# Double weights to float32: two VectorE passes in place of three

## The chip, the cores and the metric

The kernel runs on one core of a Trainium2 chip. The metric is the device time of one execution in microseconds (us); the time given is the median of three runs.

## The reference

Attention with a memory term, and behind it two feed-forward layers (called FFN here) with 2304 tokens, 512 channels and 2048 hidden columns. The weights of both layers come as doubles, everything else as float32.

```python
def reference(**kwargs):
    attn_out = _attn_ref(**attn_kwargs)                # 4 batches, 8 heads, 576 tokens, 64 wide
    B, H, S, D = attn_out.shape
    x = np.ascontiguousarray(attn_out.transpose(0, 2, 1, 3)).reshape(B * S, H * D)
    x = _moe_ref(x=x, **moe_kwargs)                    # h = x @ w_in; g = h * cos(h); g @ w_out
    return _moe2_ref(x=x, **moe2_kwargs)               # h = x @ w_in; g = h * tanh(softplus(h)); g @ w_out
```

## The kernel before

The work is cut into three parts. Attention goes over 4 batches of 4 head pairs, and each pair takes five query blocks, called steps here (80 in all). A step has a stage a (scores `sp` at L238 and L251, row minimum and mask on VectorE at L240, exp on ScalarE at L243, the reciprocal at L263, scaling at L265 on GpSimd in the first batch), a stage b two steps later (transposes `tp` at L297 and their copies `aT`), and a stage c four steps later (`o` at L313 and L324). Once per pair `memory` computes `mp` (L277), `den` (L280, L281) and `mo` (L282). When the first batch is done, units of the first layer's first half (columns of hidden, 24 matmuls `h` at L420, then cos, then 24 matmuls `y` at L478) are put between the attention steps. cos is taken for two units at once (L367, L368, L372, L375) and needs another activation table than the exp of attention, so each pair of units brings two table loads on ScalarE. After attention come the second half of the first layer, and then the second layer (`y` at L487).

The weights come in 64 pieces of 128 x 512 doubles, in four groups of 16: `w0` (needed by the units among the attention steps), `w1`, `w2` and `w3`. The function `to_f32` turns a piece into float32: a load into `wst` (two buffers), a scaling of the high words on GpSimd (the kind "ws" of `scaled`, L119), a rounding of the low words on ScalarE (L128), and three passes on VectorE (L129, L130, L133). Then `load_half` splits the float32 into a high and a low part, by a copy on ScalarE or GpSimd (L115, L119) and a subtraction on VectorE or GpSimd (L163). Of `w0` one piece is loaded at the start, and the rest from step 14 of attention on, at a rate of 0.9 pieces a step.

A scheduler of the language sets the order of the instructions on each engine, by its own estimate of their times; each engine then works through its list in order. A change of one instruction can so move others.

Of the kernel before, what the change touches and what calls it, by code (L numbers as in the profile page):

```python
# [9 lines left out]
F32 = mybir.dt.float32  # L10
F32R = mybir.dt.float32r
I32 = mybir.dt.int32
U32 = mybir.dt.uint32
AF = mybir.ActivationFunctionType
ALU = mybir.AluOpType
# [22 lines left out]


REBIAS = 2.0 ** -112  # L40


@with_exitstack
def attention_moe_moe_kernel(
# [14 lines left out]
    nc = tc.nc  # L59
    P = 128  # L60
# [21 lines left out]
    const = ctx.enter_context(tc.tile_pool(name="const"))  # L82
# [15 lines left out]
    nc.vector.reciprocal(gate, igate)  # L98
    nc.vector.tensor_scalar(omg, gate, -1.0, 1.0, ALU.mult, ALU.add)

    c_seven = const.tile([P, 1], F32, name="c_seven")
    nc.gpsimd.memset(c_seven, 7.0)

    counts = {}

    def turn_of(kind, first=False):
# [5 lines left out]
    def scaled(kind, dst, src, scale=1.0, first=False):  # L112
        eng = turn_of(kind, first)
        if eng is nc.scalar:
            eng.activation(dst, src, AF.Copy, scale=scale)  # L115
        elif scale == 1.0 and eng is nc.vector:
            eng.tensor_copy(dst, src)
        else:
            eng.tensor_scalar(dst, src, scale, 1.0, ALU.mult, ALU.mult)  # L119

    def to_f32(src, dst=None):


        st = wk.tile([P, SM, 2], I32, tag="wst", name="wst", bufs=BUFS["wst"])
        nc.sync.dma_start(st, src)
        lo, hi = st[:, :, 0], st[:, :, 1]
        scaled("ws", hi.bitcast(F32), hi.bitcast(F32), REBIAS)
        nc.scalar.activation(lo, lo.bitcast(U32), AF.Relu, scale=-(2.0 ** -29), bias=c_seven)  # L128
        nc.vector.scalar_tensor_tensor(lo, hi, 3, lo, ALU.logical_shift_left, ALU.bitwise_or)  # L129
        nc.vector.tensor_scalar(hi, hi, -(1 << 31), 7, ALU.bitwise_and, ALU.bitwise_or)  # L130
        if dst is None:
            dst = lo
        nc.vector.tensor_tensor(dst, lo, hi, ALU.bitwise_xor)  # L133
        return dst.bitcast(F32)

    def weight_pieces(win, wout, half, tl):
# [30 lines left out]
    def from_double(win, wout, half):  # L167
        def f(tl):
            for src in weight_pieces(win, wout, half, tl):
                yield to_f32(src)  # L170
        return f
# [495 lines left out]
```

## Time and profile before

| | |
|---|---|
| time, median of 3 runs (lowest, highest) | 1070.43 us (1069.86, 1070.5) |
| span of the profiled execution, first to last instruction | 1068.0 us |
| the median less the span | 2.4 us |
| TensorE (PE) busy | 1042.6 us, 98% |
| VectorE (DVE) busy | 490.7 us, 46% |
| ScalarE (ACT) busy | 485.8 us, 45% |
| GpSimd (POOL) busy | 391.6 us, 37% |

The page gives no time of its own for the profiled execution, only its span; its whole time is taken as that of the runs, the span and some 2.4 us around it. Busy shares are means over parts with different limits, so the rows below look at stretches.

### The profile page before, as it was taken

How to read it: one execution, taken by the hardware profiler on the slowest of the kernel's cores; microseconds unless marked ns; L12 is line 12 of the kernel's file. 1: busy time of each engine (PE TensorE's matmuls, PEld its weight loads, DVE VectorE, ACT ScalarE, POOL GpSimd, SP SyncE). 2: the span in 40 equal slices, each digit the busy share in tenths (PEclk: the TensorE clock that was granted, in tenths of full speed). 3: DMA queues.
4: the chain of work that ended last, by engine and by line, in shares of the span. 5: the costliest groups of instructions: out<-in, count | busy, mean ns of one | idle time of the engine just before them, and what ended most of it. 6: DMA issues, size and time to landing. Idle time of an engine off the chain costs nothing.

```text
span 1068.0 us, 17139 instructions
## 1 busy us (share of the span) xinstructions
PE 1042.6 (98%) x6512; PEld 873.7 (82%) x6512; DVE 490.7 (46%) x1136; ACT 485.8 (45%) x1023; POOL 391.6 (37%) x425
## 2 busy tenths in 40 slices
PE   6997999999999999999999999999999999999998
PEld 4666688787878899998888889888888888888897
DVE  4588885445554558776766655665000000000000
ACT  6797875556564534344535454543322321222131
POOL 3377853323232334555555555654101010110100
PEclk8999999999999999999999999999999999999999
DMA  6366642323121275425345355630300300110010
GB/s 235 119 196 224 205 135 82 119 83 122 59 87 46 73 266 190 139 90 198 110 166 177 111 176 185 228 119 22 116 1 1 118 1 0 60 40 1 21 41 20
DMA packets 66369, 116.99 MB, mean 110 GB/s; under 512 B 5616, under 2 KB 25072, under 8 KB 66288
## 3 DMA queue, kind: packets, MB, share of 16 engines
q1 hardware_dynamic: 66288, 115.91, 32.2%
q8 instruction: 51, 0.84, 0.3%
q14 instruction: 30, 0.25, 0.1%
HBM read 87.58 MB, written 28.31 MB: 109 GB/s over the span
## 4 chain that ended last, share of the span: by engine, by line
PE 92%; ACT 2%; DVE 2%; DMA 2%; issue 1%; POOL 1%; SPq 0%; DVEq 0%; POOLq 0%; ACTq 0%
PE h L420 37%; PE y L478 20%; PE y L487 18%; PE o L324 5%; PE sp L238 4%; PE tp L297 4%; PE o L313 2%; PE mp L277 1%; PE sp L251 1%; DMA qt<-in_qp_dram 1%; DMA wst<-in_w1i_dram 1%; DVE at L240 1%; ACT at L243 1%; DMA vt<-in_vn_dram 1%; POOL at L265 0%
## 5 line engine op out<-in xcount | busy, mean ns | idle before, releaser
L420 PE MATMUL h<-xbH,w 128*128 128x256 f32 (+1 forms) x1536 | 393.0, 338 | 0.1
L420 PEld LDWEIGHTS h<-xbH,w 128*128 128x128 f32 x1536 | 266.9, 190 | 33.7 <-issue 1.0
L420 PE MATMUL h<-xbL,w 128*128 128x256 f32 (+1 forms) x768 | 258.0, 336 | 1.5 <-DMA xbL<-xsL 1.5
L478 PE MATMUL y<-g,w 128*128 128x256 f32 (+1 forms) x1344 | 221.5, 319 | 4.4 <-ACT aT L115 4.2
L478 PEld LDWEIGHTS y<-g,w 128*128 128x128 f32 x1344 | 193.1, 192 | 30.8 <-issue 9.4
L487 PE MATMUL y<-w,g 128*128 128x512 f32 x864 | 201.8, 389 | 0.0
L487 PEld LDWEIGHTS y<-w,g 128*128 128x128 f32 x864 | 161.9, 188 | 33.5
L392 DVE TENSOR_TENSOR g<-e,g 128x512 fp32r<-128x512 f32 x36 | 24.9, 691 | 297.1 <-ACT g L115 297.1
L420 PEld LDWEIGHTS h<-xbL,w 128*128 128x128 f32 x768 | 145.6, 190 | 16.9 <-DMA xbL<-xsL 1.7
L392 POOL TENSOR_TENSOR g<-e,g 128x512 fp32r<-128x512 f32 x36 | 47.8, 1328 | 286.5 <-ACT g L115 286.5
L265 POOL TENSOR_SCALAR at<-at,sm,omg 128x128 f32<-128x128 f32 (+2 forms) x144 | 102.7, 723 | 134.4 <-DVE sm L263 119.2
L384 ACT ACTIVATE e<-h 128x512 f32<-128x512 f32 x72 | 43.0, 597 | 232.5 <-PE h L420 231.0
L392 POOL TENSOR_TENSOR g<-u,g 128x512 fp32r<-128x512 f32 x72 | 102.0, 1436 | 121.5 <-ACT g L115 45.6
L367 ACT ACTIVATE u<-h 128x512 int32<-128x512 f32 x72 | 42.9, 595 | 111.9 <-PE h L420 104.2
L243 ACT ACTIVATE at<-at,mn 128x128 f32<-128x128 f32 (+3 forms) x128 | 70.9, 555 | 28.2 <-DVE mn L240 26.8
L129 DVE SCALAR_TENSOR_TENSOR wst<-wst 128x512 int32<-128x512 int32 x64 | 53.9, 843 | 37.7 <-POOL wst L119 31.3
L119 POOL TENSOR_SCALAR wst<-wst 128x512 f32<-128x512 f32 x64 | 46.4, 731 | 63.2 <-DMA wst<-in_w1i_dram 25.1
L297 PE MATMUL tp<-ident,at 128*128 128x128 f32 x384 | 63.9, 285 | 5.6 <-DVE den L281 2.2
L368 DVE SCALAR_TENSOR_TENSOR u<-u,h 128x512 f32<-128x512 int32 x72 | 49.0, 682 | 40.8 <-ACT u L367 40.5
L240 DVE CUSTOM_DVE_ANT_0 at<-sp,mask 128x128 f32<-128x128 f32 (+3 forms) x128 | 59.3, 482 | 17.6 <-PE sp L238 16.0
L133 DVE TENSOR_TENSOR wst<-wst 128x512 int32<-128x512 int32 x64 | 66.1, 1035 | 1.2
L324 PE MATMUL o<-aT,vt 128*64 128x128 f32 (+1 forms) x896 | 64.5, 272 | 1.7 <-ACT aT L115 1.5
(76 smaller groups left out, 1084.1 us busy)
## 6 DMA issues: line engine op xcount, KB each, us to landing
wst<-in_w1i_dram SPq DMA_DIRECT2D x16, 512.0 KB, 5.4
wst<-in_w1o_dram SPq DMA_DIRECT2D x16, 512.0 KB, 4.6
wst<-in_w2i_dram SPq DMA_DIRECT2D x16, 512.0 KB, 4.0
wst<-in_w2o_dram SPq DMA_DIRECT2D x16, 512.0 KB, 4.7
qd<-in_qT_dram SPq DMA_DIRECT2D x16, 320.0 KB, 3.4
vt<-in_vn_dram SPq DMA_DIRECT2D x16, 320.0 KB, 3.2
xbH<-xsH SPq DMA_DIRECT2D x20, 256.0 KB, 4.9
xbL<-xsL SPq DMA_DIRECT2D x20, 256.0 KB, 4.6
```

Of the source, the lines that this page charges most:

```text
L129: nc.vector.scalar_tensor_tensor(lo, hi, 3, lo, ALU.logical_shift_left, ALU.bitwise_or)
L133: nc.vector.tensor_tensor(dst, lo, hi, ALU.bitwise_xor)
L240: nc.vector.tensor_tensor_reduce(at[:, :N], sp[:, :N], mask[:, SM - q0:SM - q0 + N], SSC, 3.0e38, ALU.add, ALU.min, mn[:, j:j + 1])
L243: marks["act"] = nc.scalar.activation(at[:, :N], at[:, :N], AF.Exp, bias=mn[:, j:j + 1], scale=-1.0, accum_out=sm[:, j:j + 1]).ins
L265: turn_of("sc", b == 0).tensor_scalar(at[:, :N], at[:, :N], sm[:, j:j + 1], gates[j], ALU.mult, ALU.mult)
L297: nc.tensor.transpose(tp[:, c:c + P], at[:, c:c + P], ident)
L324: marks["pe"] = nc.tensor.matmul(o[j * D:(j + 1) * D, :n], st["vt"][:kk, c, j * D:(j + 1) * D], a, start=False, stop=c == i, skip_group_ch ...
L368: nc.vector.scalar_tensor_tensor(u, u.bitcast(I32), -TWO_PI, h, ALU.mult, ALU.add)
L392: turn_of(kind).tensor_tensor(gL, g, gH.bitcast(F32), ALU.subtract)
L420: nc.tensor.matmul(h[:, a * T:(a + 1) * T], w_[:, c, f0:f0 + P], x_[c], start=m == 0, stop=m == 3 * NC - 1)
L478: nc.tensor.matmul(y[e // per][:, cols], w_[:, f, es], g_, start=fst and m == 0 and e % per == 0, stop=lst and m == 2, skip_group_check=True)
L487: nc.tensor.matmul(y[t], g_[:, tsl], w_[:, f, :], start=fst and m == 0, stop=lst and m == 2, skip_group_check=True)
```

## The change

The old form makes the complement of the three low mantissa bits (ScalarE: 7 less the low word, clamped at zero by Relu, rounded to an integer), ORs it with the shifted high word, makes a word with the sign and the number 7 from the high word, and XORs the two. The new form has ScalarE round the low word itself, scaled a little down so that it stays within 7; then one VectorE pass ORs the sign to it, and a second ORs the shifted high word. The pass at L130 goes, with the constant tile `c_seven`; the ScalarE operation is Copy with numbers for scale and bias where it was Relu with a bias tile.

```diff
+LOW = 29.0 / 32.0
...
-    c_seven = const.tile([P, 1], F32, name="c_seven")
-    nc.gpsimd.memset(c_seven, 7.0)
...
-        nc.scalar.activation(lo, lo.bitcast(U32), AF.Relu, scale=-(2.0 ** -29), bias=c_seven)
-        nc.vector.scalar_tensor_tensor(lo, hi, 3, lo, ALU.logical_shift_left, ALU.bitwise_or)
-        nc.vector.tensor_scalar(hi, hi, -(1 << 31), 7, ALU.bitwise_and, ALU.bitwise_or)
+        nc.scalar.activation(lo, lo.bitcast(U32), AF.Copy, scale=LOW * 2.0 ** -29, bias=0.2495)
+        nc.vector.scalar_tensor_tensor(lo, hi, -(1 << 31), lo, ALU.bitwise_and, ALU.bitwise_or)
         if dst is None:
             dst = lo
-        nc.vector.tensor_tensor(dst, lo, hi, ALU.bitwise_xor)
+        nc.vector.scalar_tensor_tensor(dst, hi, 3, lo, ALU.logical_shift_left, ALU.bitwise_or)
         return dst.bitcast(F32)
```

In the changed kernel the lines behind `to_f32` have numbers lower by 3: L420 is L417, L368 is L365, L163 is L160. The ScalarE rounding is L126, the two passes are L127 and L130. The scheduler's order differs on all engines from step 14 of attention to about step 35, and little after that: the matmuls of steps 36 to 80 stand as before but for a few.

The first place is TensorE's list where the first FFN units enter (`h` of unit one is made with the weight tiles `w_90` and `w_91` before, `w_88` and `w_89` now; unit two before with `w_94` and `w_95`). Before:

```order
L238 MATMUL sp<-kd,qd 128x256 x2
L238 MATMUL sp<-kd,qd 128x384 x2
L238 MATMUL sp<-kd,qd 128x512 x2
L420 MATMUL h<-xbH,w_90 128x256
L420 MATMUL h<-xbL,w_90 128x256
...
L251 MATMUL sp<-kd,qd 128x512
L251 MATMUL sd<-kd,qd 128x64
L420 MATMUL h<-xbH,w_94 128x256
```

Now:

```order
L417 MATMUL h<-xbH,w_88 128x256
L417 MATMUL h<-xbL,w_88 128x256
...
L294 MATMUL tp<-ident,at 128x128 x6
L310 MATMUL o<-ident,mo 128x128
L321 MATMUL o<-aT,vt 64x128 x4
L235 MATMUL sp<-kd,qd 128x384
L294 MATMUL tp<-ident,at 128x128 x8
L274 MATMUL mp<-mz,ph 128x130 x5
L310 MATMUL o<-ident,mo 128x128
```

Before, all 48 matmuls of the first two units stand between the `o` of step 21 and that of step 23. Now the first 6 (on the first half of the channels) stand there, the other 18 of unit one by step 27, and unit two at steps 32 and 33. By step 35 both lists have 72 `h` matmuls.

The second place is VectorE's list where the first `u` of cos and a pair's `mo` meet. Before:

```order
L133 TENSOR_TENSOR wst<-wst 128x512
L129 SCALAR_TENSOR_TENSOR wst<-wst 128x512
L281 RECIPROCAL den<-den 128x6
L280 SCALAR_TENSOR_TENSOR den<-mp,igate 128x4
L368 SCALAR_TENSOR_TENSOR u<-u,h 128x512
L130 TENSOR_SCALAR wst<-wst 128x512
L163 TENSOR_TENSOR w_97<-wst,w_96 128x512
L282 TENSOR_TENSOR mo<-mp,den 128x384
```

Now:

```order
L277 SCALAR_TENSOR_TENSOR den<-mp,igate 128x6
L278 RECIPROCAL den<-den 128x6
L365 SCALAR_TENSOR_TENSOR u<-u,h 128x512
L277 SCALAR_TENSOR_TENSOR den<-mp,igate 128x4
L279 TENSOR_TENSOR mo<-mp,den 128x384
L260 RECIPROCAL sm<-sm 128x1
```

Before, three weight passes and a split stand between the first `den` and `mo`; now none does.

The third place is ScalarE's list at the first cos (the sine with its table load). Before:

```order
L217 ACTIVATE ph<-qt 128x576
L328 ACTIVATE xH<-o 128x128
L218 ACTIVATE ph<-ph 128x576
L372 ACT_TABLE_LOAD
L372 ACTIVATE u<-u,c_hpi 128x1024
L115 ACTIVATE aT<-tp 128x512
```

Now:

```order
L126 ACTIVATE wst<-wst 128x512
L240 ACTIVATE at,sm<-at,mn 128x256
L214 ACTIVATE ph<-qt 128x576
L369 ACT_TABLE_LOAD
L369 ACTIVATE u<-u,c_hpi 128x1024
L325 ACTIVATE xH<-o 128x128
L126 ACTIVATE wst<-wst 128x512
L215 ACT_TABLE_LOAD
L215 ACTIVATE ph<-ph 128x576
L240 ACTIVATE at,sm<-at,mn 128x256
L113 ACTIVATE aT<-tp 128x512
```

The first cos came with step 23 and comes with step 33 now; the number of table loads is the same, and behind the sine stands the exp of the next pair's `ph`, with a rounding of weights ahead of it, before the copy `aT`.

## Rows read from the trace of the kernel before

**Rows 1.** The page's first part: busy us (share of the span) and instructions.

```profile
PE 1042.6 (98%) x6512; PEld 873.7 (82%) x6512; DVE 490.7 (46%) x1136; ACT 485.8 (45%) x1023; POOL 391.6 (37%) x425
```

**Rows 2.** Windows, cut at the ends of head pairs: length, busy us by engine, granted clock, DMA.

```profile
35.00:50.20 15.20, 15.20 (x122) 9.93 (x122) 7.44 (x34) 11.37 (x38) 5.51 (x9) 1.00 0.36 109
50.20:69.20 19.00, 18.27 (x147) 12.60 (x148) 14.98 (x51) 15.77 (x48) 10.55 (x14) 1.00 0.60 203
69.20:83.30 14.10, 13.68 (x119) 9.24 (x117) 13.06 (x48) 12.50 (x38) 11.90 (x13) 1.00 0.64 200
83.30:111.10 27.80, 22.37 (x180) 18.30 (x180) 22.28 (x69) 20.12 (x50) 20.12 (x22) 0.94 0.66 222
111.10:127.70 16.60, 15.18 (x126) 10.34 (x124) 16.50 (x56) 13.18 (x40) 12.53 (x15) 1.00 0.55 179
127.70:145.30 17.60, 17.33 (x151) 13.71 (x152) 15.68 (x51) 14.10 (x40) 13.58 (x16) 1.00 0.53 177
145.30:400.00 254.70, 250.52 (x2125) 213.16 (x2124) 134.25 (x433) 139.71 (x344) 80.65 (x102) 0.99 0.32 106
400.00:1068.00 668.00, 664.09 (x3395) 569.55 (x3394) 248.88 (x327) 235.39 (x362) 224.38 (x194) 1.00 0.27 93
...
1050.00:1075.00 25.00, 14.35 (x77) 12.11 (x75) 0.69 (x1) 3.65 (x6) 1.28 (x1) 0.94 0.06 21
```

**Rows 3.** Windows of line L130 alone: length, DVE busy (instructions), clock, DMA.

```profile
480.00:650.00 170.00, 19.55 (x16) 1.00 0.45 155
```

**Rows 4.** Chain that ended last, 155 to 170 us: start, us, what.

```profile
162.84 2.88 PE h L420 x24
```

**Rows 5.** Waits of TensorE, 83 to 112 us: total us, times, longest.

```profile
PE tp L297 <- DVE den L281: 2.2, 1, 2.2
PE h L420 <- DMA xbL<-xsL: 1.5, 1, 1.5
PE o L313 <- ACT aT L115: 0.9, 1, 0.9
```

**Rows 6.** Windows, 104 to 108 us: columns as in rows 2.

```profile
104.00:106.00 2.00, 1.17 (x6) 0.95 (x8) 2.00 (x5) 1.99 (x4) 1.40 (x2) 0.71 0.47 137
106.00:108.00 2.00, 2.00 (x19) 1.67 (x16) 2.00 (x7) 0.28 (x1) 1.45 (x2) 0.50 0.22 47
```

**Rows 7.** Groups by line of VectorE, 50 to 150 us: busy us, mean ns, idle before.

```profile
L133 DVE TENSOR_TENSOR wst<-wst 128x512 int32<-128x512 int32 x16 | 12.5, 784 | 0.1
L129 DVE SCALAR_TENSOR_TENSOR wst<-wst 128x512 int32<-128x512 int32 x16 | 11.6, 723 | 2.8 <-POOL wst L119 2.3 <-ACT wst L128 0.6
L130 DVE TENSOR_SCALAR wst<-wst 128x512 int32<-128x512 int32 x16 | 9.5, 594 | 0.0
```

**Rows 8.** The tile wst: duration ns min/median/max, first and last start.

```profile
L130 DVE TENSOR_SCALAR wst<-wst x64: 404/654/1543, 57.5 to 735.1; 128x512 int32<-128x512 int32 x64
L133 DVE TENSOR_TENSOR wst<-wst x64: 678/732/1790, 57.9 to 735.6; 128x512 int32<-128x512 int32 x64
```

**Rows 9.** Groups by line of ScalarE, 50 to 150 us: columns as in rows 7.

```profile
L128 ACT ACTIVATE wst<-wst,c_seven 128x512 int32<-128x512 uint32 x16 | 12.3, 772 | 3.0 <-DMA wst<-in_w1o_dram 1.6 <-DMA wst<-in_w1i_dram 1.4
...
L115 ACT ACTIVATE w<-wst 128x512 fp32r<-128x512 f32 x8 | 5.4, 679 | 4.2 <-DVE wst L133 4.2
```

**Rows 10.** Timeline of VectorE, 96 to 104 us: start, us, what.

```profile
100.18 0.68 DVE L129 SCALAR_TENSOR_TENSOR wst<-wst 128x512 int32<-128x512 int32 x1
...
101.51 0.42 DVE L130 TENSOR_SCALAR wst<-wst 128x512 int32<-128x512 int32 x1
101.85 0.68 DVE L163 TENSOR_TENSOR w<-wst,w 128x512 fp32r<-128x512 f32 x1
102.45 0.55 DVE L282 TENSOR_TENSOR mo<-mp,den 128x384 f32<-128x384 f32 x1
```

**Rows 11.** Timeline of ScalarE, 88 to 112 us: start, us, what, idle before.

```profile
101.85 1.28 ACT L372 ACT_TABLE_LOAD   x1
103.14 1.15 ACT L372 ACTIVATE u<-u,c_hpi 128x1024 f32<-128x1024 f32 x1
```

## The prediction

> **What bounds the kernel now.** The page's first part says TensorE: 98% busy, VectorE 46% [rows 1]. A share of the span hides where the two meet, so the next view is the windows, cut at the ends of head pairs [rows 2]. From 400 us on TensorE is busy for 664.09 of 668.00 us, and 3.65 of the missing 3.91 us lie behind its last matmul: it stops at 1064.35 us (14.35 us into the last window), and the span ends at 1068.0. Three of the four groups of weights are converted in that stretch. Between 480 and 650 us, for instance, the 16 passes of L130 take 19.55 us of VectorE [rows 3], over twice what 16 take early, and TensorE loses nothing by it. So 48 of 64 pieces are hidden behind matmuls, and their saving is worth zero; if that cover were gone, VectorE would set the pace there, but it is busy for 248.88 of those 668 us and loses work by the change. From 145.30 to 400 us no weights are converted; the 4.18 us that TensorE idles there stand, since its order there is kept.
>
> What is left is the five head pairs from 50.20 to 145.30 us, in which the 16 pieces of `w0` are converted among attention steps. In these windows VectorE is busy for 82.5 of 95.1 us (14.98 + 13.06 + 22.28 + 16.50 + 15.68), 87%, and TensorE idles 0.73 + 0.42 + 5.43 + 1.42 + 0.27 = 8.27 us. The pair before, without weight passes, takes 15.20 us with VectorE at 7.44 us, 49%, and TensorE never idle. Five such pairs and the 72 `h` matmuls that the order puts among them (24 take 2.88 us [rows 4]) would be 76.0 + 8.6 = 84.6 us, 10.5 less than the 95.1 us that they take. Idle time makes 8.27 of this. Most of the rest is the clock: the granted clock fell to 0.71 from 104 to 106 us and to 0.50, its lower level of 1.2 GHz, from 106 to 108 [rows 6], behind the waits of [rows 5]; that costs 2.00 x 0.29 + 2.00 x 0.50 = 1.58 us. **At stake are 8.27 + 1.58 = 9.85 us**, and 5.43 + 1.58 of it in the one window from 83.30 to 111.10 us. The waits there name a VectorE instruction of `den` (2.2 us), a load of `xbL` (1.5) and a copy `aT` (0.9) [rows 5]. VectorE worked without a gap then: between the two `den` and the `mo` that TensorE needed stood L129, L130 and the split L163, 0.60, 0.34 and 0.60 us from start to next start [rows 10] (for L129 its 0.68 us less the overlap of 0.08 that L163 shows). Behind them ScalarE's table load and sine (1.28 + 1.15 us [rows 11]) kept `aT` back.
>
> **The change, part by part.** (a) *The pass L130 goes*: 16 in the stretch at a mean of 594 ns, 9.5 us of VectorE [rows 7]. The Trainium skill (VectorE: DVE Perf Modes, The perf-mode tier table) speaks against so much: a float32 operation with one tensor source in SBUF runs at twice the rate of one with two, so the pass that goes would be the cheapest of the three. The trace agrees for its fastest, 404 ns against 678 for L133 [rows 8]; by it alone the saving would be 16 x 0.404 = 6.5 us and the gain under (e) 0.2 us smaller. I take the mean, since passes are stretched up to 1.5 us in place.
>
> (b) *XOR of two tensors becomes shift-and-OR*: the trace has no such second pass. Its nearest rows are L133 itself (784 ns) and L129, the same form (723) [rows 7]: 16 x 0 to 0.061 = 0 to 1.0 us. I take 1.0, as the form is L129's.
>
> (c) *ScalarE's rounding without a bias tile*: bounded by 772 ns as now and by the 679 ns of the Copy at L115 on the same tile [rows 9]: 0 to 1.5 us of 16. I take 1.5, the like operation; ScalarE has room, so it counts for the latency of a piece only. GpSimd's scaling and the loads stay as they are; the memset of `c_seven` goes before the first matmul has its data, and counts nothing.
>
> (d) *Latency*: from ready words to the float32 piece, three passes of 723 + 594 + 784 ns become two of 723 at most 784 ns: 0.65 us less, so one of the two `wst` buffers and the next load come as much earlier.
>
> (e) *Worth of the VectorE time*: 82.5 - 9.5 - 1.0 = 72.0 of 95.1 us, 76%. TensorE's idle time goes with VectorE's load: nil at 49%, 8.27 us at 87%. On a line between the two, 76% gives 8.27 x 27 / 38 = 5.9 us, a fall of 29%. In the four quieter windows (0.73 + 0.42 + 1.42 + 0.27 = 2.84 us) that is **0.8 us**. The bounds are 0 (idle time set by other engines) and 2.84.
>
> (f) *The order at the first units*. The scheduler, with shorter conversions, no longer puts 48 `h` matmuls, both `u`, the sine and three conversions into one pair. The second half of `xbL` is needed three steps later, some 9 us at 15.20 us for five: the 1.5 us wait goes. `mo` now stands ahead of the weight passes: 0.60 + 0.34 + 0.60 = 1.5 of the 2.2 us wait go. The wait for `aT` may stay or move with the sine. That is **3.0 us**. With the idle stretch so cut, the clock may or may not fall; I count half of 1.58, **0.8 us**. Bounds: 0, if as much idle time turns up at step 33, and 5.43 + 1.58 = 7.01.
>
> Sum: 0.8 + 3.0 + 0.8 = 4.6 us, between 0 and 9.85. The profiled span is 1068.0 us and the runs' median 1070.43, so 2.4 us lie around the span and stay. **1070.43 - 4.6 = 1065.8 us.**
>
> **Rivals.** *Hidden anyway.* VectorE is at 46% and TensorE at 98%: what is gone from VectorE was never on the path, and the early waits are a matter of loads and of table loads, which the change doesn't touch. For it: 48 of 64 pieces are hidden so, and one of three waits named is a DMA. Against: VectorE's 87% in the five pairs, and the passes between `den` and `mo`. It gives 0.8 us or less, 1070 us. The Trainium skill (Perfetto Trace Analysis, Identifying the Most-Contended Engine) says to work on the engine with the highest occupancy first, which would here be TensorE; by it nothing is gained. The trace bears this out from 145 us on and not before.
>
> *The stall moves and grows (slower).* Around the first sine ScalarE now has, in order, a rounding of weights, a table load, the sine, `xH`, another rounding, a second table load and the exp of `ph`, ahead of the next exp of scores. If the load of either piece comes late, ScalarE stands with the scores' exp behind it, VectorE's `sm` and GpSimd's scaling wait for that, and TensorE for the scaled rows. Priced by the stall that is there now, 5.43 + 1.58 us, plus the 1.28 + 1.15 us of load and sine that the six `h` matmuls left at step 23 no longer cover, against 7.0 us that go with the old place: +2.4 us, 1072.9. It decides where the piece lands later than TensorE's filler lasts (24 `h`, 2.88 us). For it: TensorE had 48 `h` matmuls (5.8 us) at the old place and stalled still. Against: the order has unit three close behind, and VectorE has less to do.
>
> *Everything goes.* With VectorE at 76% the five pairs run as the undisturbed one: 9.85 us less, 1060.6. Against: each pair with weights has some idle time, and the table loads stay.
>
> *No cheaper in fact*: two two-source passes stretched as L133 is (784 ns) instead of three: 16 x 0.061 = 1.0 us of VectorE less saved; by (e) under 0.1 us, inside the forecast.
>
> **The numbers.** The forecast holds with 0.48 (1062 to 1068.2), everything goes with 0.12, hidden 0.27 (1068.3 to 1072), slower 0.13 (1072.6 and up, centred at 1072.9 and open above). A difference of 0.2%, 2.1 us, is about what a measurement of this kernel can tell from none. So faster has 0.60, same 0.27, slower 0.13. The range leaves out the far half of everything-goes and most of slower: 1061.2 to 1072.0.
>
> **What would show it.** In the trace of the changed kernel: 16 pairs of passes of some 0.7 us each and VectorE near 72 us in the stretch up to step 35 ((a), (b)); the rounding near 0.68 us (c); TensorE's idle time from 50 us to step 35 at 4 to 5 us in place of 8.3 (e, f); no wait for `xbL` at the first units, and the clock at 1.00 or a shorter fall (f); from there on every matmul earlier by the same amount to the end. I am wrong if the idle time is as large at another place, such as the sine at step 33, if the clock falls twice, or if the 4.18 us of idle time from 145.30 to 400 us change, which I hold fixed.

## The result and the profile after

The changed kernel takes 1080.86 us (median of 5 runs, 1079.3 to 1082.22) where the kernel before, run beside it, takes 1070.5 (5 runs, 1069.86 to 1073.4): a ratio of 1.0088, with a 95% interval of 1.0072 to 1.0105. It is slower by 0.9%, outside the predicted range. The profiled execution has a span of 1079.6 us, 11.6 longer. Every median here is of runs within 1.5% of the fastest of their kernel; one run of 2594 us (the changed operations in their own order with two places, below) is left out so, and with it that median would be 1081.77 us in place of 1080.29. In the changed kernel the load of a piece is L123, and the `y` matmul of L478 is L475.

The page's first part, the line that answers to [rows 1], columns as there:

```profile
PE 1049.2 (97%) x6512; PEld 876.3 (81%) x6512; DVE 452.8 (42%) x1072; ACT 480.3 (44%) x1023; POOL 392.2 (36%) x424
```

VectorE lost 37.9 us of work, as the edit promised, and the kernel still got longer. Where, the windows of the changed kernel show, cut at the ends of the same head pairs (for [rows 2]), and in steps of 2 us behind 466 us (for [rows 6]):

```profile
36.20:51.40 15.20, 15.20 (x122) 9.95 (x121) 7.42 (x34) 11.36 (x38) 6.05 (x9) 1.00 0.41 131
51.40:69.50 18.10, 18.10 (x147) 12.75 (x146) 13.51 (x50) 14.84 (x46) 9.84 (x13) 1.00 0.59 180
69.50:87.60 18.10, 14.17 (x110) 9.01 (x111) 14.60 (x47) 13.77 (x42) 12.81 (x14) 0.96 0.57 187
87.60:106.20 18.60, 18.60 (x143) 13.86 (x142) 14.15 (x45) 11.30 (x34) 11.56 (x17) 0.86 0.73 238
106.20:125.00 18.80, 17.33 (x140) 11.91 (x139) 17.15 (x56) 15.02 (x46) 15.18 (x17) 1.00 0.56 182
125.00:149.70 24.70, 23.28 (x169) 17.63 (x168) 19.34 (x58) 17.85 (x44) 15.35 (x17) 0.93 0.53 166
149.70:176.80 27.10, 26.47 (x227) 22.64 (x226) 15.20 (x48) 14.37 (x35) 10.85 (x14) 1.00 0.36 115
...
400.00:1079.60 679.60, 671.35 (x3439) 576.11 (x3437) 216.24 (x285) 232.83 (x363) 229.03 (x196) 1.00 0.29 94
...
466.00:468.00 2.00, 0.98 (x9) 0.78 (x7) 2.00 (x4) 0.73 (x2) 1.27 (x2) 1.00 0.03 8
468.00:470.00 2.00, 0.31 (x1) 0.19 (x1) 2.00 (x3) 0.00 (x0) 0.97 (x2) 1.00 0.10 10
470.00:472.00 2.00, 1.04 (x8) 0.99 (x8) 1.84 (x3) 0.13 (x1) 1.64 (x2) 0.96 0.78 208
472.00:474.00 2.00, 2.00 (x11) 2.00 (x11) 1.41 (x2) 1.97 (x4) 1.84 (x2) 0.50 0.86 306
474.00:476.00 2.00, 2.00 (x14) 2.00 (x14) 1.97 (x4) 0.23 (x1) 0.39 (x2) 0.69 0.58 168
```

Two things are to be seen. The long window of the kernel before, 27.80 us, shrank to 18.60 (part of its matmuls stand in later windows now), but the window ahead of it grew from 14.10 to 18.10 with 3.93 us of idle TensorE, and the clock is below 1.00 in three windows where it was in one (two falls, the first from 86 to 94 us and the second from 144 to 148). And the stretch that the prediction called hidden has a hole: from 466 to 472 us TensorE works 2.33 of 6 us, and then the clock stands at 0.50 and 0.69. The waits of TensorE name who was late, from 50 to 177 us (first four lines, for [rows 5]) and from 440 to 480 us (last two), columns as there:

```profile
PE tp L294 <- POOL at L262: 2.6, 4, 1.1
PE sp L235 <- ACT aT L113: 1.7, 2, 0.9
PE o L321 <- ACT aT L113: 1.5, 1, 1.5
PE sp L235 <- DVE mn L237: 0.9, 1, 0.9
...
PE y L475 <- DVE g L115: 2.7, 1, 2.7
PE y L475 <- POOL g L389: 1.0, 1, 1.0
```

Setting the n-th matmul of each kind beside the n-th of the kernel before, the changed kernel is 1.3 us behind at 25 to 60 us, 7.0 at 175, 5.2 from 213 (the kernel before runs at a clock of 0.88 and 0.78 from 200 to 210 us, the changed one does not), 4.4 at 450, 10.1 from 480 and 11.7 from 745 us to the end.

The groups by line of the stretch from 50 to 150 us, VectorE for [rows 7] and ScalarE for [rows 9]:

```profile
L130 DVE SCALAR_TENSOR_TENSOR wst<-wst 128x512 int32<-128x512 int32 x15 | 12.6, 837 | 0.0
L127 DVE SCALAR_TENSOR_TENSOR wst<-wst 128x512 int32<-128x512 int32 x15 | 12.1, 809 | 7.2 <-POOL wst L117 5.0 <-ACT sm L259 1.9 <-ACT wst L126 0.2
...
L126 ACT ACTIVATE wst<-wst 128x512 int32<-128x512 uint32 x16 | 10.8, 678 | 8.8 <-DMA wst<-in_w1i_dram 3.8 <-DMA wst<-in_w1o_dram 3.4 <-POOL at L262 1.5
```

The rounding is as short as forecast (678 ns), but ScalarE now waits 7.2 us in these 16 for the load of the words, where it waited 3.0 us [rows 9]. That is the first hint of the cause: the loads come later. The piece at 460 us shows it in full, in the timelines of the changed kernel by engine (start, duration, instruction, idle time before it):

```profile
457.89 1.64 POOL L160 TENSOR_TENSOR w<-wst,w 128x512 fp32r<-128x512 f32 x1
...
459.15 0.93 DVE L160 TENSOR_TENSOR w<-wst,w 128x512 fp32r<-128x512 f32 x1 [0.80 <-ACT w L113]
...
460.14 0.37 SPq L123 DMA_DIRECT2D wst<-in_w1i_dram  x1
...
463.95 0.69 ACT L126 ACTIVATE wst<-wst 128x512 int32<-128x512 uint32 x1 [3.86 <-DMA wst<-in_w1i_dram]
464.53 1.15 ACT L369 ACTIVATE u<-u,c_hpi 128x1024 f32<-128x1024 f32 x1
...
466.41 1.27 DVE L372 TENSOR_TENSOR u<-h,u 128x512 f32<-128x512 f32 x2
467.61 1.60 DVE L127 SCALAR_TENSOR_TENSOR wst<-wst 128x512 int32<-128x512 int32 x1
...
469.69 0.35 PE L475 MATMUL y<-g,w 128*128 128x256 f32 x1 [2.71 <-DVE g L115]
```

Both splits of the pieces ahead have ended at 459.53 and 460.08 us; the next load is issued at 460.14 and lands some 3.8 us later; ScalarE has the rounding of that piece ahead of the sine L369 in its list and stands for 3.86 us; the product at L372, the cast `g` and TensorE's `y` are late in turn. VectorE adds to it: between that product and the cast stands the pass L127 of the next piece, 1.60 us long here.

In the early stretch the trace is less plain. The load issued at 77.48 us lands at 82.63; ScalarE has stood for 1.55 us and begins the rounding at 82.71, with an exp and the copy `aT` behind it, for which TensorE waits 1.5 us. But a scaling of `at` on GpSimd that the same rounding waits for ends at 82.65, so this wait alone does not tell which of the two cost the time. The experiments have to.

### The profile page after: what moved, and what is told of

Read it like the earlier page. It is cut to its first block, busy times and chain, and to the rows that moved or that the text cites. A ratio compares the mean times of both kernels' runs of the same rounds, so it can differ in the third digit from the quotient of the medians.

```text
span 1079.6 us, 17195 instructions
## 1 busy us (share of the span) xinstructions
PE 1049.2 (97%) x6512; PEld 876.3 (81%) x6512; DVE 452.8 (42%) x1072; ACT 480.3 (44%) x1023; POOL 392.2 (36%) x424
## 4 chain that ended last, share of the span: by engine, by line
PE 77%; DMA 8%; DVE 6%; ACT 5%; POOL 3%; issue 2%; SPq 0%; POOLq 0%; ACTq 0%; DVEq 0%
PE h L417 30%; PE y L475 16%; PE y L484 15%; PE o L321 4%; PE sp L235 4%; PE tp L294 3%; DMA wst<-in_w1o_dram 2%; DMA wst<-in_w2o_dram 2%; DVE wst L127 2%; PE o L310 1%; DVE wst L130 1%; DMA wst<-in_w1i_dram 1%; PE mp L274 1%; DMA wst<-in_w2i_dram 1%; ACT at L240 1%
## 5 line engine op out<-in xcount | busy, mean ns | idle before, releaser
L417 PE MATMUL h<-xbH,w 128*128 128x256 f32 (+1 forms) x1536 | 392.8, 338 | 0.0
L417 PEld LDWEIGHTS h<-xbH,w 128*128 128x128 f32 x1536 | 267.2, 190 | 33.0 <-issue 1.2
L417 PE MATMUL h<-xbL,w 128*128 128x256 f32 (+1 forms) x768 | 258.2, 337 | 0.0
L475 PE MATMUL y<-g,w 128*128 128x256 f32 (+1 forms) x1344 | 221.3, 319 | 8.5 <-ACT aT L113 4.2
L475 PEld LDWEIGHTS y<-g,w 128*128 128x128 f32 x1344 | 193.0, 192 | 34.6 <-issue 11.9
L417 PEld LDWEIGHTS h<-xbL,w 128*128 128x128 f32 x768 | 145.9, 190 | 15.3 <-issue 0.2
L389 DVE TENSOR_TENSOR g<-e,g 128x512 fp32r<-128x512 f32 x36 | 25.9, 718 | 299.2 <-ACT g L113 268.6
L389 POOL TENSOR_TENSOR g<-e,g 128x512 fp32r<-128x512 f32 x36 | 47.3, 1313 | 281.2 <-ACT g L113 281.2
L389 POOL TENSOR_TENSOR g<-u,g 128x512 fp32r<-128x512 f32 x72 | 103.3, 1452 | 99.0 <-DVE g L115 40.9
L117 POOL TENSOR_SCALAR wst<-wst 128x512 f32<-128x512 f32 x64 | 46.8, 731 | 138.8 <-DMA wst<-in_w2o_dram 40.7
L365 DVE SCALAR_TENSOR_TENSOR u<-u,h 128x512 f32<-128x512 int32 x72 | 49.0, 682 | 65.1 <-ACT u L364 64.8
L127 DVE SCALAR_TENSOR_TENSOR wst<-wst 128x512 int32<-128x512 int32 x64 | 54.4, 851 | 44.5 <-POOL wst L117 41.6
L235 PE MATMUL sp<-kd,qd 64*128 64x128 f32 (+3 forms) x256 | 65.5, 495 | 7.0 <-DMA kd<-in_kT_dram 4.5
L126 ACT ACTIVATE wst<-wst 128x512 int32<-128x512 uint32 x64 | 43.0, 674 | 64.7 <-DMA wst<-in_w1i_dram 17.0
```

What stands on the lines that cost most here:

```text
L127: nc.vector.scalar_tensor_tensor(lo, hi, -(1 << 31), lo, ALU.bitwise_and, ALU.bitwise_or)
L235: nc.tensor.matmul(sp[:, :N], st["q"][rows, q0:q0 + P], st["k"][rows, :N], start=True, stop=True)
L365: nc.vector.scalar_tensor_tensor(u, u.bitcast(I32), -TWO_PI, h, ALU.mult, ALU.add)
L389: turn_of(kind).tensor_tensor(gL, g, gH.bitcast(F32), ALU.subtract)
L417: nc.tensor.matmul(h[:, a * T:(a + 1) * T], w_[:, c, f0:f0 + P], x_[c], start=m == 0, stop=m == 3 * NC - 1)
L475: nc.tensor.matmul(y[e // per][:, cols], w_[:, f, es], g_, start=fst and m == 0 and e % per == 0, stop=lst and m == 2, skip_group_check=True)
```

## The experiments

### Is it the order?

First theory: the operations are cheaper as meant, and the scheduler's new order costs the time. To test it, an order can be written out: behind the traced program each instruction of an engine is tied behind the one that is to stand ahead of it there. The ranks come from the built programs of the two kernels, without or with the pass at L130.

```diff
         attention_moe_moe_kernel(tc, *args)
+        in_order(tc)
...
+        for d in ranks[at:at + len(mine)]:
+            r += d
+            want.append(mine[r])
+        for a, b in zip(want, want[1:]):
+            tc.add_manual_dep(b, a.name, mybir.DependencyInfo(mybir.DependencyClass.NoSync, mybir.DependencyReason.DATA), reason="order")
```

The changed operations in the order of the kernel before:

> The changed kernel's operations, with the order of the kernel before written out for all five engines (every instruction behind the one that stood ahead of it there; the sign pass left out). If the new order is what cost the time (theory), this run shows the operations alone: 1064 to 1068 us, and neither the idle 2.7 us for the cast g at 470 us nor the idle 3.9 us of TensorE at 69 to 88 us comes back. If the new operations themselves cost it (rival: the two-source passes stretched beside GpSimd, or a shorter VectorE chain that shifts the bursts), it stays at 1078 to 1082.

Measured: 1069.45 us, ratio to the kernel before 0.9982 (0.9972 to 0.9992), a little above the range expected. The operations as such cost nothing.

The old operations in the changed kernel's order:

> The operations of the kernel before (Relu, three VectorE passes), with the order of the changed kernel written out for all five engines; the sign pass stands right behind the first pass. Theory (order): slow like the changed kernel or slower, 1078 to 1086 us, since the same order now carries 38 us more of VectorE work, and TensorE waits for g at 460 to 476 us. Rival (operations): 1068 to 1073, as before.

Measured: 1094.55 us, 1.0212 (1.0192 to 1.0232), slower than the range expected. Up to here the theory holds. The two orders agree on all engines between TensorE's instructions 893 and 2460, so that the first part can be taken from one and the rest from the other:

> The changed kernel's operations; the order of the kernel before up to where both orders coincide (TensorE's instruction 1500, about 260 us), its own order behind that. Theory: the loss of about 5.6 us between 50 and 165 us goes and that at 460 to 476 us (about 5.7) and at 725 to 750 us (1.6) stays: 1073 to 1076 us. If the first loss belongs to the operations: 1079 to 1082.

> The reverse: the changed kernel's own order up to TensorE's instruction 1500 (about 260 us), the order of the kernel before behind that. Theory: the idle time and the lower clock at 466 to 476 us and the wait at 725 to 750 us go (5.7 + 1.6 us), those at 50 to 165 us stay: 1072 to 1075 us. If the later losses belong to the operations: 1079 to 1082.

Measured: 1069.3 us, 0.9980 (0.9966 to 0.9994), and 1072.66 us, 1.0011 (0.9999 to 1.0023). The theory falls with the first of them. It has the changed kernel's order at 460 and at 745 us, and neither loss is there: TensorE is busy for 40.00 of 40 us from 440 to 480. Either half of the old order takes that loss away, so it isn't a property of the order at that place. Something that the kernels of longer time share had to be looked for.

It is the loads of the pieces. The numbers are from the traces: the issue of the n-th load less the end of the split of piece n - 2, in us, for six of the 64 pieces (counted from 0).

```
piece             14      20      25      29      31      63
before         -3.25   -6.10  -12.44  -11.02   -8.14   -8.74
changed        +0.03   +0.07   +0.03   +0.61   +0.03   +0.03
```

In the changed kernel every load waits for the split two pieces ahead of it; before, loads go out up to 22 us ahead of it: 50 of 60 by more than 1 us, and the other 10 within about 1 us of its end. The built programs say why. The 64 staging tiles `wst` stand at these addresses of a partition (and so many tiles at each):

```
before     82048 (18)  86144 (17)  90240 (15)  94336 (14)
changed    82048 (33)  86144 (31)
```

The code asks for two buffers (`bufs=2`) in both. That number steers the scheduler's plan; what the loads wait for on the chip, by the issue times above, is the reuse of an address, and the placement, which is worked out anew for each build, had given the kernel before four addresses. The runs above agree: four places in the two of 1069.45 and 1069.3 us, two in the others (1094.55 and 1072.66), since an imposed order changed the placement too. Other tiles lost places as well (`mn` from 5 to 2, `den` and `qt` from 4 to 2, `xL` from 10 to 5).

### Is it the places?

Second theory: four places of staging became two. The staging tiles are made once and used in turn, so that their number is fixed, and the scheduler is left free; rivals are the operations, and the other tiles.

```diff
+    staging = [const.tile([P, SM, 2], I32, name=f"wst{n}") for n in range(4)]
+    staged = []
...
-        st = wk.tile([P, SM, 2], I32, tag="wst", name="wst", bufs=BUFS["wst"])
+        st = staging[len(staged) % 4]
+        staged.append(0)
```

> The changed kernel with four staging tiles wst made once and used in turn; the scheduler sets the order. In the traces so far each load of a piece is issued 0.03 us after the split of the piece two before it ends in the two slow kernels (changed; old operations in the new order), and up to 21 us ahead of that end in the three others. Theory now (staging depth: two places in memory in the changed kernel, four before): 1062 to 1070 us, loads issued ahead, TensorE's idle time and lower clock at 69 to 88 and 466 to 476 us gone. Rival 1 (the new operations or their order): 1076 to 1082. Rival 2 (other tiles that also lost places, mn, den, qt, xL): between.

> Control for the run with four: the same edit with two staging tiles; here the tiles mn and den keep as many places as in the kernel before (5 and 4). Theory (staging depth alone): 1077 to 1085, each load issued right behind the split two pieces earlier. Rival 2 (the other tiles): 1066 to 1071.

> The kernel before with two staging tiles made once; its operations are unchanged. Theory: slow, 1082 to 1095 us, as in the run of the old operations in the new order (1094.6), with a wait for g in the stretch of the feed-forward at 440 to 480 us. Rival 1 (the new operations are to blame): 1069 to 1073.

> The kernel before with four staging tiles made once: the control. Theory: 1067 to 1073, as before; against the changed kernel with four stages it gives what the operations alone are worth, by the order-pinned run about 2 us. Rival 1: the changed kernel with four stages is the slower of the two.

Measured: the changed kernel with four 1082.26 us, 1.0095 (1.0078 to 1.0111), with two 1077.16, 1.0046 (1.0028 to 1.0063); the kernel before with two 1079.94, 1.0072 (1.0054 to 1.0091), with four 1093.68, 1.0201 (1.0181 to 1.0220). Two places make the kernel before slow, as expected, if less than expected (1082 to 1095). Both expectations for four failed by over 10 us. Their loads are early indeed (up to 57 us ahead), but the scheduler now plans with four and draws more conversions forward: VectorE begins the 16th piece at 116 us in place of 150, and the first `h` comes at 120 us in place of 91. TensorE waits behind them. Its waits from 50 to 150 us (first two lines) and from 440 to 460 us in the changed kernel with four (in the runs with staging tiles made once, lines outside `to_f32` have the numbers of the kernel before; the load is L126, the rounding L129, the passes L130 and L133 in runs with the changed operations):

```profile
PE o L313 <- DVE mo L282: 3.7, 1, 3.7
PE tp L297 <- POOL at L265: 3.6, 3, 3.0
...
PE y L478 <- DVE yp L117: 3.5, 1, 3.5
```

So places and plan are two things, and the runs so far had changed both at once.

### Order and places apart

Both edits together: the order written out, and the staging tiles fixed.

> The changed kernel's operations with its own order written out for all engines, and four staging tiles made once and used in turn instead of two places: order kept, places doubled. If places are what was lost (theory): 1068 to 1072 us, each load ahead of the split two pieces earlier, TensorE's wait for g at 466 to 472 us gone. If the order alone is what costs (rival): 1079 to 1083, as the changed kernel.

> The changed kernel's operations in the order of the kernel before, with two staging tiles: order as in the run at 1069.5 us, places halved. Theory (places): 1075 to 1082. Rival (order): 1068 to 1071.

> Control: the changed kernel's operations in the order of the kernel before, with four staging tiles made once. Both theories: 1067 to 1071, as the order-pinned run (1069.5); it tells whether making the tiles once costs or gives anything by itself.

> Control: the changed kernel's operations in its own order, with two staging tiles made once; the tiles mn and den have five and four places here, as in the kernel before, where the changed kernel has two and two. If staging places and order are all: 1079 to 1083, as the changed kernel. If the places of mn and den count: 1074 to 1078.

Measured, all with the changed operations (ratio to the kernel before, 95% interval):

| | two places | four places |
|---|---|---|
| order of the changed kernel | 1080.29 us, 1.0084 (1.0059 to 1.0110) | 1066.99 us, 0.9962 (0.9948 to 0.9975) |
| order of the kernel before | 1074.48 us, 1.0023 (1.0007 to 1.0040) | 1068.84 us, 0.9974 (0.9957 to 0.9991) |

This settles it. With operations and order as in the changed kernel, two more places give back 13.3 us, and the kernel is then faster than the one before. For the changed operations the order costs nothing: with four places the new one is no slower than the old. It is only more sensitive to the places (13.3 us against 5.6, the latter from 1074.48, just under the range expected). The other tiles are placed anew in each of these builds too, but they don't go with the time: with two places for `wst` and 1080.29 us, `mn` and `den` have five and four places as in the kernel before, and with four places for `wst` and 1066.99 us, `den` has two and `xL` four, as few as in the changed kernel or fewer.

The hole at 466 us comes back with the two places, as the window of that run shows, to be read against the last line of the next fence:

```profile
440.00:480.00 40.00, 35.99 (x277) 35.48 (x276) 32.24 (x41) 13.90 (x22) 24.23 (x22) 0.91 0.43 134
```

The same matmuls in the same order, with four places: the windows, cut at the ends of the same pairs, to be read against those of the changed kernel above.

```profile
50.30:68.30 18.00, 18.00 (x147) 12.71 (x146) 13.81 (x50) 16.12 (x49) 10.43 (x14) 1.00 0.65 224
68.30:83.20 14.90, 13.19 (x114) 9.04 (x113) 13.94 (x48) 12.58 (x39) 11.81 (x13) 1.00 0.57 168
83.20:100.10 16.90, 16.12 (x141) 11.97 (x140) 13.80 (x45) 10.98 (x34) 11.63 (x16) 1.00 0.81 270
100.10:118.20 18.10, 16.80 (x138) 11.52 (x137) 16.68 (x56) 14.67 (x45) 15.57 (x17) 1.00 0.62 211
118.20:139.60 21.40, 20.59 (x167) 15.83 (x164) 18.97 (x58) 17.54 (x43) 14.03 (x15) 1.00 0.53 172
139.60:166.60 27.00, 26.82 (x228) 22.98 (x229) 14.98 (x48) 15.03 (x37) 13.02 (x17) 1.00 0.36 113
...
440.00:480.00 40.00, 40.00 (x296) 38.22 (x296) 25.44 (x36) 13.76 (x22) 20.47 (x19) 1.00 0.33 108
```

The six pairs take 116.3 us in place of 125.4. TensorE idles 4.78 us instead of 7.45, and its clock stays at 1.00, where the changed kernel loses by estimate 18.10 x 0.04 + 18.60 x 0.14 + 24.70 x 0.07 = 5.1 us to it. That is 7.7 of the 9.1 us; the rest is not to be read from these rows. By the n-th matmul the changed kernel loses 1.2 us ahead of 50 us, 8.7 from there to 165 us, 5.6 at 460 to 476 and 1.6 at 745; a fall of the clock around 260 us in the run with four places gives 1.5 back.

ScalarE's rounding in the run with four places, the group by line from 50 to 150 us, waits for loads as little as in the kernel before:

```profile
L129 ACT ACTIVATE wst<-wst 128x512 int32<-128x512 uint32 x16 | 10.9, 684 | 2.6 <-DMA wst<-in_w1o_dram 2.0 <-DMA wst<-in_w1i_dram 0.6
```

### What the operations are worth, and how many places it takes

> The operations of the kernel before, in the order of the changed kernel, with four staging tiles. Against the changed operations in the same order and with the same places (1067.0 us) this prices the operations alone. If the predicted sum holds (4.6 us): 1070 to 1073 us. If the operations are worth only the 2 us that the two orders of the kernel before gave: 1068 to 1070. With two places this order took 1094.6 with the old operations: places alone would then be worth over 20 us here.

> Order and places as in the run at 1067.0 us, with ScalarE's old rounding (Relu with the bias tile, which is computed for the old passes, so that the values differ) ahead of the two new VectorE passes. By the predicted sum ScalarE's part is worth little over zero (0.09 us for each of the pieces, off the path): 1066 to 1068. If the shorter rounding is a large part of the gain: 1068 to 1071.

> The changed operations in the changed kernel's own order with three staging tiles. If each further place gives back a like part of the 14.8 us between two places (1081.8) and four (1067.0): about 1074. If one more place already covers a load's 3.5 to 4 us ahead of its use: 1066 to 1070.

Measured: the old operations in the changed kernel's order with four places 1074.94 us, 1.0043 (1.0027 to 1.0058), above both ranges expected; the VectorE half alone 1066.77, 0.9967 (0.9952 to 0.9982); three places 1065.82, 0.9957 (0.9939 to 0.9974). With 1080.29 us for two places, the 14.8 us of the last expectation are 13.3.

At equal order and places the operations are worth 7.9 us in the order made for them (1074.94 less 1066.99; 8.7 by the ratios, as the two runs were on different chips). In the order made for the old ones they are worth 0.18% (the first run of all, 2 us). Places alone are worth 19.6 us to the old operations in that order (1094.55 less 1074.94; 18 by the ratios). To the old operations the new order does cost something, 4.4 us at four places (1074.94 against 1070.54). The ScalarE half has no share that can be measured. And three places do what four do; this run, 4.7 us under the kernel before, has the lowest time of all, with the changed kernel's own order, though its interval overlaps that of four.

The waits of the load queue show the step from two places to three and four. The lines are waits of the queue's loads for a split on VectorE or GpSimd (total us, times, longest): first the kernel before,

```profile
SPq L125 <- DVE w L163: 37.9, 6, 14.2
SPq L125 <- POOL w L163: 30.8, 13, 4.4
```

then the changed kernel,

```profile
SPq L123 <- DVE w L160: 92.9, 22, 9.8
...
SPq L123 <- POOL w L160: 82.3, 28, 4.9
```

its order with three places,

```profile
SPq L126 <- DVE w L163: 43.7, 14, 7.8
SPq L126 <- POOL w L163: 41.3, 14, 3.9
```

and with four.

```profile
SPq L126 <- POOL w L163: 23.3, 9, 3.9
SPq L126 <- DVE w L163: 23.3, 7, 6.0
```

Fifty such waits of 175 us together became 28 of 85 us with one more place, and 16 of 47 us with two. Waits put down to the VectorE pass ahead of the split are not counted in (25 us in the kernel before, 49 in the changed one). A queue's wait is no loss by itself: 19 of 69 us in the kernel before and 28 with three places cost nothing that shows. It is one where, as at 460 us, the load's 3.8 us then lie between the split of one piece and the rounding of the next, with a sine behind that rounding.

## Why the prediction was wrong

**What bounds the kernel.** The five pairs were the right place for the gain, but "48 of 64 pieces are hidden behind matmuls, and their saving is worth zero" was guarded against one loss of that cover only, VectorE setting the pace, and VectorE had less to do. The cover was lost by a late load, at 460 us: TensorE stood for 3.7 us and ran below full clock for 4, 5.7 us together by the n-th matmul.

**(a), (b): mis-sized.** The pass went, but the two that are left take 809 and 837 ns in the stretch, not 723 and at most 784: with the run at four places (842 and 825 ns, the lines below) 16 x 1.667 = 26.7 us in place of the 33.6 us of [rows 7]. That is 6.9 us less, where 9.5 + 1.0 = 10.5 were forecast.

```profile
L130 DVE SCALAR_TENSOR_TENSOR wst<-wst 128x512 int32<-128x512 int32 x16 | 13.5, 842 | 5.6 <-POOL wst L119 5.1 <-issue 0.3 <-ACT wst L129 0.2
L133 DVE SCALAR_TENSOR_TENSOR wst<-wst 128x512 int32<-128x512 int32 x16 | 13.2, 825 | 0.0
```

**(c) was right**: 678 ns, and worth nothing measurable, as the run with the VectorE half alone shows.

**(d) is the step that failed**, with the clause under (c) that "the loads stay as they are". It counts on "one of the two `wst` buffers" coming free earlier, and the next load with it. The kernel before had two buffers in its code and four places in memory, and the change halved them: the loads came later, each behind the split two pieces ahead, and that cost 13.3 us by the runs with two and four places. The code said two, so the number was taken from there; the trace of before had the answer. Of its loads 50 of 60 go out 1 to 22 us ahead of the end of the split that two buffers would have to wait for.

**(e)** VectorE's load did not fall to 76%, and by itself it does not set the idle time. With four places VectorE is busy for 77.2 of the 89.3 us of the five pairs, 86%, as before (87%), and TensorE idles 4.60 us in place of 8.27. Where the operations alone change (the first run: old order, four places), VectorE has 5.5 us less to do from 50 to 165 us. The line of (e) would give about 1.0 us for that (an estimate: 8.27 x 4.7 / 38, for 82.1% to 77.4%). TensorE's busy time in the window is the same, with 8 matmuls more, and by the n-th matmul it gains 1.3 us from 58 to 165 us. So the small size was about right, and the larger gain of the order made for these operations is not a matter of the load. The window of the kernel before,

```profile
50.00:165.00 115.00, 106.73 (x879) 81.44 (x879) 94.43 (x307) 87.00 (x239) 77.27 (x87) 0.99 0.57 187
```

and that of the first run:

```profile
50.00:165.00 115.00, 106.78 (x887) 81.10 (x885) 88.97 (x294) 86.43 (x242) 76.33 (x88) 0.99 0.58 187
```

What counts there is which instruction waits, not the share.

**(f)** With the places kept it happened as forecast: no wait for `xbL`, the clock at 1.00, no window over 21.40 us, idle time "at 4 to 5 us" (4.60). In the changed kernel the idle time turned up one pair earlier, in two later pairs and behind the sine at 464 us, and behind 50 us the clock fell three times, which the prediction had named as a sign that it was wrong.

**The sum.** With three places in the same order the time is 1065.82 us, and the forecast was 1065.8. That is in part luck. Against the profiled kernel before, the run with three places gains 2.6 us up to 170 us, 1.5 from a fall of the clock at 202 us that the prediction held fixed, and 0.8 around 440 us. Nor did the gain split as the sum has it: the sum gives the order 3.8 us and the lighter VectorE 0.8, but the order with the old operations and four places costs 4.4 us, and the operations give back 7.9 in it. In the old order they are worth 2 us, so most of the gain comes only with both.

**The rivals.** "The stall moves and grows" is what came, by its own mechanism (a rounding ahead of the sine in ScalarE's list whose load is late), and its condition, a piece that lands later than TensorE's filler lasts, was met: at 460 us, not at the first sine, and at 5.7 us, not 2.4. It had a chance of 0.13, and 1080.86 us lies in its open interval. Its price looked at one place alone. It did not see what would make loads late everywhere.

**What stays open.** Why the placement gave two places is a matter of the build and was not tried on the chip. Each half of the change by itself was built too, and gave two and three places; nothing in the edit's own operations asks for it.

## What to carry to other kernels

A count of buffers in the code is what a plan was made with, not what the chip has: read the depth from the trace, by the issue of load n against the last use of piece n - 1, n - 2 and so on, before and after any change, however small, since a placement worked out anew can halve it. When orders and timings all move at once, write the order out and fix the buffers, one at a time; half an order, as in the third and fourth run, shows when the cause is elsewhere. The Trainium skill (Trainium Kernel Development and Optimization, Best Practices) advises to double-buffer so that loads overlap with compute; by the runs here two places were too few where every piece, once loaded, passes GpSimd, ScalarE and VectorE before its place is free (1080.3 us with two, 1065.8 with three), and planning with more of them was no cure by itself (1082.3).

## What the runs showed of the hardware

Holes in TensorE's work cost twice. Behind the idle time at 466 to 472 us the granted clock was 0.50 and 0.69 for 4 us (0.50 is the lower level, 1.2 GHz), and behind that at 69.5 to 87.6 us it was 0.86 over the next 18.6 us. In the same order with four places, where no window of that stretch has more than 1.71 us of idle time, it stayed at 1.00 throughout. In the kernel before, 1.39 us of idle time at 202 to 204 us were followed by a clock of 0.50 at 204 to 206 us. In the changed kernel 1.47 us of idle time, spread over 106 to 125 us, were followed by no fall before 144 us.

A VectorE pass over 128x512 integers with two tensor sources took from 664 ns to 1.81 us in the changed kernel. The long ones around 460 us (1.78 us from 455.52, 1.60 from 467.61) lie beside work of GpSimd (L389, L117, L160); whether that is the cause was not tried.
